# Down stage of a transformer block: loads ordered by hand on one queue, operands two products ahead, and a warmed start

## Chip, cores, metric

One core of a Trainium2 chip. The metric is the device time of one launch in microseconds (us). Profiles show the span from the first to the last instruction, which is about 1.8 us shorter than the time of the same execution.

## The reference

A block with linear attention and a gated feed-forward layer, batch 1, 2048 tokens, width 1024, hidden width 3584, all in bf16:

```python
h  = x + linear_attention(layernorm(x), wqkv) @ wo      # 32 heads of 32
g  = layernorm(h)
gate, up = g @ W_gate, g @ W_up
h2 = h + (gate * (gate > 0) * up) @ W_down              # the "down stage" is this product
```

## The kernel before

All large products use Strassen's scheme, seven products for eight. The down stage does it on two levels. Outside there are seven products of halves. Two of them are "plain" (112 matmuls of 512 columns, 24.2 us); five are "inner", that is again seven groups of 28 matmuls of 256 columns (3.06 us a group, 21.4 us in all). VectorE makes the operand sums of the next inner product (`t1` to `t4` from weights, `s1` to `s4` from hidden activations) between its other work: a *snapshot* adds a base to the running accumulator, a *sink* adds a finished accumulator to a snapshot, adds h and sends it out.

```python
OUTER = (1, 2, 6, 5, 7, 3, 4)
INNER = (2, 6, 5, 3, 4)          # 1 and 7 are plain
...
    def acc(tag):                # PSUM: A twice, X and Y once, two banks each
        return accs.tile([P, 2 * NW], FP32, tag=tag, bufs=2 if tag == "A" else 1, name="acc" + tag)
...
            cur["m1"]()
            ...
            cur["s1"]()          # snapshot of group 1
            cur["m2"]()
            if prv: prv["m4"]()  # groups of the product before, left over
            late_x()
            cur["00"]()          # sink of group 2
            pop()                # one operand sum of the next product
            ...
            late_w()
            pop()
            cur["m6"]()
            if prv: prv["01"]()
            pop()
            cur["m5"]()
            cur["s2"]()          # snapshot of group 6: frees the accumulator for group 7
            pop(2)
            cur["m7"]()
            pop(2)
            if tail:             # the last product
                cur["snap"]("u3", 1, 1)
                cur["snap"]("u3f", 1, 0)
                cur["m4f"]()
                cur["11"]()
                cur["m3"]()
                cur["10f"]()
                cur["01a"]()
                cur["01b"]()
```

Loads, h loads too, are issued from SyncE's queue when the scheduler puts them there, one product ahead.

Of the kernel before, what the change touches and what calls it, by code (L numbers as in the profile page):

```python
# [31 lines left out]
def block_kernel(ctx: ExitStack, tc: tile.TileContext, x, wqkv, wo, wg, wu, wd, out, H: int):  # L32
    nc = tc.nc
    P = 128
# [44 lines left out]
    PE_T = 4  # L79
    XB, HB = 3, 2  # L80
# [129 lines left out]
    with ExitStack() as actx:  # L210
# [36 lines left out]
        def ln_T(t):  # L247
# [13 lines left out]
            xn = bwork.tile([P, D], BF16, tag="hn", bufs=HB, name="xn")  # L261
            nc.vector.scalar_tensor_tensor(out=nmr, in0=mv[:, 0:1], scalar=-1.0, in1=rstd, op0=ALU.mult, op1=ALU.mult)
            nc.scalar.activation(out=xn[:], in_=x_sb[:], func=ACT.Identity, bias=nmr, scale=rstd)
            if t not in atiles[:PE_T]:
                nc.sync.dma_start_transpose(out=xT[s][i][:, :, r:r + P], in_=xn[:])
                return
            for k in range(2):
                pt = pspool.tile([P, KH, P], BF16, tag="D", bufs=1, name="tp")
                for kc in range(KH):
                    nc.tensor.transpose(pt[:, kc, :], xn[:, (k * KH + kc) * P:(k * KH + kc + 1) * P], ident[:])  # L270
                (nc.scalar.copy if k else nc.vector.tensor_copy)(
                    out=xT[s][i][:, k * KH:(k + 1) * KH, r:r + P], in_=pt[:])
# [93 lines left out]
        ln_T(atiles[0])  # L366
# [42 lines left out]
    abpool = abctx.enter_context(tc.tile_pool(name="abpool", bufs=3, space=PSUM, side="right"))  # L409
# [21 lines left out]
    with tc.tile_pool(name="qwork0", bufs=2, side="right") as pool:  # L431
        qw.append(pool)
        for c in range(0, KH, 2):
            for _ in q_unit(0, c):
                pass
    xctx[0].close()
    q1ctx = ExitStack()
    qw.append(q1ctx.enter_context(tc.tile_pool(name="qwork1", bufs=2, side="right")))
# [7 lines left out]
    def new_hn(s):  # L446
        aops = mctx.enter_context(tc.tile_pool(name=f"aops{s}", bufs=1))
        hnT.append([aops.tile([P, KC, SW], BF16, name=f"hn{s}{i}") for i in range(2)])
        hns.append([aops.tile([P, KH, SW], FP16, name=f"hs{s}{k}") for k in range(3)])

    new_hn(0)
    wpool = mctx.enter_context(tc.tile_pool(name="wpool", bufs=2))
# [3 lines left out]
    def load_group(g):  # L456

        tiles, loads = [], []
        for nm, v in (("wg", wg_v), ("wu", wu_v)):
            w_sb = wpool.tile([P, KC, 2, GP * P], BF16, tag=nm, name=nm)  # L460
# [108 lines left out]
    tpool = mctx.enter_context(tc.tile_pool(name="tpool", bufs=2))  # L569
    mwork = mctx.enter_context(tc.tile_pool(name="mwork", bufs=2))  # L570
# [33 lines left out]
    def wd_sums(c):  # L604
# [4 lines left out]
        def load():  # L609
            st["raw"] = raw = spool[0].tile([P, 2, 2, D], BF16, tag="wraw", bufs=1, name="wraw")  # L610
            for k in range(2):
                nc.sync.dma_start(out=raw[:, k], in_=wd_k[:, k, 2 * c:2 * c + 2, :])
            st["b"] = [[raw[:, k, :, j * DW:(j + 1) * DW] for j in range(2)] for k in range(2)]

        def one():
            st["t"] = spool[0].tile([P, 4, 2, DW], FP16, tag="wt", bufs=1, name="wt")
# [14 lines left out]
        return [load, one, two, three, four]  # L631
# [21 lines left out]
    def early_sums(f):  # L653
# [10 lines left out]
        return [load, lambda: None, lambda: hh_sums_a(st[0], 0, f), lambda: hh_sums_b(st[0], 0, f)]  # L664
# [56 lines left out]
    prepool = ctx.enter_context(tc.tile_pool(name="prepool", side="right", **reuse))  # L721
# [61 lines left out]

    runs = [(early[f // GP], f, f % GP, [1]) for f in range(NE)]
    runs += [(g, g * GP + fi, fi, [0, 1]) for g in range(NE // GP, FH // GP) for fi in range(GP)]
    fill = [p for f in range(NE) for p in early_sums(f)] + [p for c in range(FH // 2) for p in wd_sums(c)]
# [23 lines left out]
    for r, (wt, f, fi, toks) in enumerate(runs):  # L810
        w = [ops() for _, ops in now]
        later = []
        for n, s in enumerate(toks):
# [8 lines left out]
            if r >= NE:  # L822
                want = len(fill) // (nwin - k) if nwin - k > 1 else len(fill)
                want = min(len(fill), max(want, 0))
# [41 lines left out]
            if k == nwin - 1:  # L866
                b11 = [prepool.tile([P, FQ, DW], BF16, tag="b11", name="b11")]
                nc.sync.dma_start(out=b11[0][:], in_=wd_v[:, 0:FQ, 0:DW])
    assert not fill

    HW = DW // 2
    raws = {1: (0, 0), 2: (1, 0), 3: (1, 1)}
    sums_of = {4: 3, 5: 0, 6: 1, 7: 2}
    xslot = {2: H12, 3: S4, 4: H22, 5: S1, 6: S2, 7: S3}
    OUTER = (1, 2, 6, 5, 7, 3, 4)
    INNER = (2, 6, 5, 3, 4)
    outs = {2: (0, 0), 7: (1, 1), 3: (0, 1), 4: (1, 0)}
    full = slice(0, DW)
    ALL = slice(0, NT)

    def plain_mm(ps, x, w, p, kh):
        s, t0 = divmod(2 * p, NT)
        for t in range(2):
            for f in range(FQ):
                nc.tensor.matmul(ps[:, t * NW:(t + 1) * NW], lhsT=x[s][kh][:, f, (t0 + t) * P:(t0 + t + 1) * P],  # L885
                                 rhs=w[kh][:, f, :], start=(kh == 0 and f == 0),
                                 stop=(kh == 1 and f == FQ - 1), skip_group_check=True)

    first_ps = [acc("A")]
    wfirst = [b11[0][:], None]  # L890
    xfirst = [[t[:] for t in row] for row in x1]
    plain_mm(first_ps[0], xfirst, wfirst, 0, 0)
# [11 lines left out]
    dpool = ctx.enter_context(tc.tile_pool(name="dpool", **reuse))  # L904

    def load_half(op, x):

        k = op["k"]
        w = dpool.tile([P, FQ, DW], BF16, tag="w", bufs=4, name="w")
        if k in raws:  # L910
            i, j = raws[k]
            nc.sync.dma_start(out=w[:], in_=wd_v[:, i * FH + x * FQ:i * FH + (x + 1) * FQ, j * DW:(j + 1) * DW])
        else:
            nc.sync.dma_start(out=w[:].bitcast(FP16), in_=t_dram[sums_of[k]][:, x * FQ:(x + 1) * FQ, :])
        op["wt"][x] = w
        op["w"][x] = w[:] if k in raws else w[:].bitcast(FP16)

    def load_x(op, s, kh):

        k = op["k"]  # L920
        t = (x1pool if op["n"] % 2 == 0 else dpool).tile([P, FQ, SW], BF16, tag="x", bufs=4, name="x")
        nc.sync.dma_start(out=t[:], in_=x_dram[s][kh][:, xslot[k], :, :])
        op["xt"][s][kh] = t
        op["x"][s][kh] = t[:].bitcast(FP16) if k in (3, 5, 6, 7) else t[:]

    def new_op(n):
        return {"n": n, "k": OUTER[n], "wt": [None] * 2, "w": [None] * 2,
                "xt": [[None] * 2 for _ in range(2)], "x": [[None] * 2 for _ in range(2)], "s": {}, "t": {}}

    queue = []  # L930
# [10 lines left out]
    def queue_sums(op):  # L941
# [4 lines left out]
        def a(i, j):  # L946
            return op["x"][i][j]

        def b(i, j):
            return op["w"][i][:, :, j * HW:(j + 1) * HW]  # L950

        def new_s(nm):
            S[nm] = dpool.tile([P, FQ, SW], FP16, tag="xs", bufs=4, name="xs")[:]
# [11 lines left out]
        def t3():  # L965
            T["t3"] = op["wt"][0][:].bitcast(FP16)[:, :, HW:DW]
# [11 lines left out]
        def s3():  # L978
            S["s3"] = op["xt"][1][0][:].bitcast(FP16)
# [5 lines left out]
        queue.extend((op, f.__name__, f) for f in (t1, s1, s2, t2, s3, t3, t4, s4))  # L985
# [8 lines left out]
    def load_h(k, s):  # L994

        if k in outs:
            i, j = outs[k]
            v = dpool.tile([P, NT, DW], BF16, tag="h", bufs=3, name="h")
            nc.sync.dma_start(out=v[:], in_=h_dram[i][s][:, :, j * DW:(j + 1) * DW])
            hres[k, s] = v  # L1000

    def put(k, s, ts, cs, ps, m):

        i, j = outs[k]
        o = dpool.tile([P, NT * HW], BF16, tag="o", bufs=3, name="o")
        ov = o[:, 0:(ts.stop - ts.start) * (cs.stop - cs.start)].rearrange("p (t d) -> p t d", t=ts.stop - ts.start)
        add(out=ov, in0=ps, in1=m, op=ALU.add)  # L1007
        add(out=ov, in0=ov, in1=hres[k, s][:, ts, cs], op=ALU.add)
# [9 lines left out]
    def inner(op):  # L1018
# [4 lines left out]
        def left(m):  # L1023
            return {1: op["x"][0][0], 2: op["x"][0][1], 3: op["s"].get("s4"), 4: op["x"][1][1],
                    5: op["s"].get("s1"), 6: op["s"].get("s2"), 7: op["s"].get("s3")}[m]

        def right(m):
            w = op["w"]
# [6 lines left out]
        def mm(m, nm, t=None):  # L1035
# [4 lines left out]
            for tt in range(NT):  # L1040
# [9 lines left out]
        def sink(s, j, nm, m, ts=ALL):  # L1050
# [3 lines left out]
            else:  # L1054
                put(k, s, ts, cols(j), view(nm)[:, ts], m)
# [8 lines left out]
            "01a": lambda: sink(0, 1, "E", "u2", slice(0, 2)), "01b": lambda: sink(0, 1, "E", "u2", slice(2, 4)),  # L1064
            "m7f": lambda: snap("u3f", 1, 0),
# [3 lines left out]
    op = ops[0]  # L1069
    op["w"][0], op["x"] = b11[0][:], xfirst  # L1070
    load_half(op, 1)
    for n in range(1, 2):
        load_half(ops[n], 0)
        load_half(ops[n], 1)
        for s, kh in ((1, 0), (1, 1), (0, 0), (0, 1)):
            load_x(ops[n], s, kh)
# [7 lines left out]
    for p in range(1, 4):  # L1084
        plain_mm(pss[p], op["x"], op["w"], p, 0)
    for p in range(4):
        plain_mm(pss[p], op["x"], op["w"], p, 1)
        sink1(p, pss[p])
        if p >= 1:
            pop(2)  # L1090
    load_h(OUTER[1], 0)
    load_h(OUTER[1], 1)
    pop(8)

    prv = None
    for n in range(1, len(OUTER)):
# [4 lines left out]
        def early_loads():  # L1101
            if nxt:
                load_half(nxt, 0)
                for s, kh in ((1, 0), (0, 0), (0, 1)):
                    load_x(nxt, s, kh)
                load_h(nxt["k"], 0)

        def late_x():
            if nxt:
                load_x(nxt, 1, 1)  # L1110

        def late_w():
            if nxt:
                load_half(nxt, 1)
                if nxt["k"] in INNER:
                    queue_sums(nxt)

        early_loads()
        if op["k"] in INNER:
# [21 lines left out]
            if nxt:  # L1141
                load_h(nxt["k"], 1)
            cur["m5"]()
            cur["s2"]()
            pop(2)
            cur["m7"]()
            pop(2)
            if tail:
                cur["snap"]("u3", 1, 1)
                cur["snap"]("u3f", 1, 0)  # L1150
                cur["m4f"]()
                cur["11"]()
                cur["m3"]()
                cur["10f"]()
                cur["01a"]()
                cur["01b"]()
# [3 lines left out]
        else:  # L1160
            pss = []
            for p in range(4):
                ps = acc(("A", "A", "XY"[n % 2], "XY"[(n + 1) % 2])[p])
                plain_mm(ps, op["x"], op["w"], p, 0)
                plain_mm(ps, op["x"], op["w"], p, 1)
                if p == 0 and prv:
# [6 lines left out]
                    prv["01"]()  # L1173
                s, t0 = divmod(2 * p, NT)
# [5 lines left out]
            if nxt:  # L1180
                load_h(nxt["k"], 1)
# [47 lines left out]
```

## Time and profile before

| | before |
|---|---|
| time, median of 3 | 763.67 us (763.53 to 764.01) |
| profiled execution | 762.83 us, span 761.0 us, mean clock 0.996 |
| TensorE busy | 721.2 us, 95% |
| first matmul of the down stage | 583.74 us |
| last matmul ends, last addition of VectorE ends | 755.6, 757.8 us |

The prediction shows the lines that bear on the start and the down stage. Two more rows of TensorE's timeline are needed later, from the stretch where attention hands over to gate and up (start, length, engine, line, output and inputs, shape, count, and in brackets the wait before it with what ended it; a row without brackets followed its predecessor without a wait):

```profile
272.38 1.02 PE L673 MATMUL Aq<-hs,tu 128*128 128x512 f16 x4 [1.65 <-ACT m L152]
...
297.12 1.03 PE L753 MATMUL accA<-hn,wg 128*128 128x512 bf16 x4
```

The second is the first matmul of the main gate and up stage. From there to 583 us TensorE never waits as long as 0.4 us, so a lead or a lag at 297 us is carried to the down stage unchanged.

### The profile page before, as it was taken

The numbers are of one execution on the slowest core, as the hardware profiler recorded it, in microseconds if no ns is written. First come the engines' busy times: TensorE is split into PE (matmuls) and PEld (weight loads), VectorE is DVE, ScalarE is ACT, GpSimd is POOL, SyncE is SP. The second block draws the span as 40 slices with busy tenths as digits, with TensorE's granted clock in tenths as the row PEclk, the third lists the DMA queues.
The fourth block names the chain that finished last, engine by engine and source line by source line (L and its number), as shares of the span: only waits on it lengthen the run. The fifth ranks groups of instructions, "written<-read, shape, count | busy, mean of one in ns | idle before, by whom it ended". The sixth has DMA issues, their size and how long they took to land.

```text
span 761.0 us, 10554 instructions
## 1 busy us (share of the span) xinstructions
PE 721.2 (95%) x3951; PEld 381.3 (50%) x4004; DVE 565.7 (74%) x1022; ACT 326.5 (43%) x597; POOL 6.1 (1%) x44
## 2 busy tenths in 40 slices
PE   5999999999889989999999999999999879999996
PEld 2443555444344434444444444444444358875685
DVE  5997654787896767687777877788776279947995
ACT  4876553878768554444444444444434010000000
POOL 0000000000000000000000000000000000000000
PEclk9999999999999999999999999999999999999999
DMA  9665002079767544166438356495543899967713
GB/s 318 153 138 152 1 1 107 5 165 224 193 160 183 121 118 145 42 180 185 147 105 246 102 157 221 165 279 178 177 172 122 292 405 333 362 236 255 266 29 97
DMA packets 146419, 132.03 MB, mean 173 GB/s; under 512 B 50880, under 2 KB 127936, under 8 KB 146368
## 3 DMA queue, kind: packets, MB, share of 16 engines
q1 hardware_dynamic: 138928, 127.16, 55.3%
q10 hardware_dynamic: 7440, 4.20, 1.9%
q8 instruction: 31, 0.51, 0.3%
q14 instruction: 20, 0.16, 0.1%
HBM read 79.95 MB, written 39.85 MB: 157 GB/s over the span
## 4 chain that ended last, share of the span: by engine, by line
PE 65%; DVE 16%; DMA 9%; ACT 5%; issue 2%; SPq 1%; POOL 0%; DVEq 0%; ACTq 0%
PE accA L753 22%; PE accX L753 8%; PE accY L753 8%; DMA x<-x_dram 5%; PE accA L1042 4%; PE attn L517 4%; PE Aq L285 3%; PE Aq L419 2%; PE Eq L285 2%; PE Aq L673 2%; PE accX L1042 2%; PE accY L1042 2%; DVE stats L254 2%; DVE o L1007 1%; DMA hn<-hn 1%
## 5 line engine op out<-in xcount | busy, mean ns | idle before, releaser
L763 ACT ACTIVATE gu<-gu 128x512 bf16<-128x512 bf16 x72 | 45.4, 631 | 122.3 <-DVE gu L762 122.3
L758 ACT COPY snap<-accA 128x1024 f32<-128x1024 f32 x72 | 72.7, 1010 | 44.9 <-PE accA L753 44.8
L517 PE MATMUL attn<-wo_mem,oT 128*128 128x512 bf16 x247 | 57.3, 379 | 4.1 <-DVE o_sb L497 3.4
L753 PEld LDWEIGHTS <-tg 128*128 128x128 f16 x384 | 37.6, 98 | 45.3
L753 PEld LDWEIGHTS <-tu 128*128 128x128 f16 x384 | 37.6, 98 | 45.3
L1042 PEld LDWEIGHTS <-x 128*128 128x128 f16 (+1 forms) x560 | 54.6, 98 | 9.9 <-DMA out_dram<-o 1.3
L152 ACT COPY u<-Aq 128x512 f32<-128x512 f32 x56 | 32.2, 581 | 44.9 <-PE Aq L285 21.3
L762 DVE TENSOR_TENSOR gu<-accY,snap 128x1024 bf16<-128x1024 f32 x36 | 43.9, 1220 | 10.2 <-ACT snap L758 10.2
L753 PE MATMUL accA<-hn,tg 128*128 128x512 f16 (+1 forms) x192 | 49.3, 379 | 0.0
L753 PE MATMUL accA<-hn,tu 128*128 128x512 f16 (+1 forms) x192 | 49.3, 379 | 0.0
L762 DVE TENSOR_TENSOR gu<-accX,snap 128x1024 bf16<-128x1024 f32 x36 | 43.9, 1220 | 7.0 <-ACT snap L758 3.9
L1042 PEld LDWEIGHTS <-xs 128*128 128x128 f16 x420 | 41.7, 99 | 11.1 <-issue 5.7
L753 PEld LDWEIGHTS <-wg 128*128 128x128 bf16 x288 | 28.2, 98 | 34.0
L753 PEld LDWEIGHTS <-wu 128*128 128x128 bf16 x288 | 28.2, 98 | 34.0
L517 PEld LDWEIGHTS <-oT 128*128 128x128 bf16 x256 | 24.9, 97 | 34.9 <-issue 6.7
L885 PEld LDWEIGHTS <-x 128*128 128x128 bf16 (+1 forms) x224 | 21.9, 98 | 29.2 <-issue 3.3
L1042 PE MATMUL accA<-w,x 128*128 128x256 f16 (+1 forms) x280 | 31.7, 273 | 1.0 <-DVE snap L1048 0.7
L766 DVE TENSOR_TENSOR hq<-gu 128x512 bf16<-128x512 bf16 x48 | 20.3, 423 | 14.9 <-ACT gu L763 14.9
L285 PEld LDWEIGHTS <-xT 128*128 128x128 bf16 (+1 forms) x192 | 18.6, 98 | 24.9 <-issue 3.4
L497 DVE TENSOR_TENSOR o_sb<-nd,rd 128x384 bf16<-128x384 f32 (+1 forms) x48 | 22.8, 507 | 8.6 <-ACT rd L496 8.3
L1048 DVE TENSOR_TENSOR snap<-accA,u 128x1024 f32<-128x1024 f32 x16 | 19.4, 1219 | 11.5 <-PE accA L1042 11.5
L519 DVE SCALAR_TENSOR_TENSOR x_res<-attn,x_res 128x512 bf16<-128x512 f32 x32 | 22.0, 688 | 6.3 <-PE attn L517 6.2
(199 smaller groups left out, 1368.4 us busy)
## 6 DMA issues: line engine op xcount, KB each, us to landing
x<-x_dram SPq DMA_DIRECT2D x24, 896.0 KB, 7.2
x_dram<-hq SPq DMA_DIRECT2D x28, 512.0 KB, 3.1
wg<-in_B_W_gate_dram SPq DMA_DIRECT2D x14, 512.0 KB, 5.0
wu<-in_B_W_up_dram SPq DMA_DIRECT2D x14, 512.0 KB, 7.2
wraw<-in_B_W_down_dram SPq DMA_DIRECT2D x14, 512.0 KB, 4.9
x_dram<-hq SPq DMA_DIRECT2D x28, 256.0 KB, 3.0
t_dram<-wt SPq DMA_DIRECT2D x28, 256.0 KB, 2.2
w<-t_dram SPq DMA_DIRECT2D x8, 896.0 KB, 8.4
```

The costliest lines, as they stand in the source:

```text
L152: nc.scalar.copy(out=snaps[nm, v], in_=A[v][:])
L285: nc.tensor.matmul(ps[:], lhsT=left[m - 1][:, kc, r + v * P:r + (v + 1) * P], rhs=right[m - 1][:, kc, :], start=(start and kc == 0), stop= ...
L497: nc.vector.tensor_tensor(out=ov[:, c0:c0 + n], in0=ndv[:, :, 0:P].rearrange("p k (h e) -> p k h e", h=HPC), in1=rd[:, 0:n, :].unsqueeze(3 ...
L517: nc.tensor.matmul(ps[:], lhsT=st["oT"][:, c, :], rhs=wo_sb[:, c, j * NW:(j + 1) * NW], start=(c == 0), stop=(c == KC - 1))
L519: nc.vector.scalar_tensor_tensor(out=h_sb[:, j * NW:(j + 1) * NW], in0=ps[:], scalar=1.0, in1=h_sb[:, j * NW:(j + 1) * NW], op0=ALU.mult, ...
L753: nc.tensor.matmul(ps[:, v, :], lhsT=w[v][n - 1][:, kc, :], rhs=left[n - 1][:, kc, :], start=(t is not None and kc == 0), stop=(kc == KH - ...
L758: nc.scalar.copy(out=st[nm][:], in_=halves(st["A"]))
L762: add(out=g[:], in0=halves(st[nm]), in1=st[base][:], op=ALU.add)
L763: nc.scalar.activation(out=g[:, 0, :], in_=g[:, 0, :], func=ACT.Relu)
L766: add(out=out[q], in0=st[q][:, 0, :], in1=st[q][:, 1, :], op=ALU.mult)
L885: nc.tensor.matmul(ps[:, t * NW:(t + 1) * NW], lhsT=x[s][kh][:, f, (t0 + t) * P:(t0 + t + 1) * P], rhs=w[kh][:, f, :], start=(kh == 0 and ...
L1042: nc.tensor.matmul(pv[:, tt, :], lhsT=left(m)[:, f, tt * P:(tt + 1) * P], rhs=right(m)[:, f, :], start=(t is not None and f == 0 and tt % ...
```

## The change

The intent: no load on the path of the down stage. Its parts, cut to the core:

```diff
 # start
+        with tc.high_priority():
+            zero = asmall.tile([P, NW], BF16, tag="zero", bufs=1, name="zero")
+            nc.vector.memset(zero[:], 0.0)
+            spin = pspool.tile([P, NW], FP32, tag="E", bufs=2, name="spin")
+            for n in range(16):
+                nc.tensor.matmul(spin[:], lhsT=zero[:, 0:P], rhs=zero[:], start=True, stop=True)
+            ln_T(atiles[0])        # first tile: normalised on VectorE in two halves
 # pools of the middle: waits tile by tile; staging of the weight sums in two buffers
-    mwork = mctx.enter_context(tc.tile_pool(name="mwork", bufs=2))
+    mwork = mctx.enter_context(tc.tile_pool(name="mwork", reuse_waits="tile", bufs=2))
-            st["raw"] = raw = spool[0].tile([P, 2, 2, D], BF16, tag="wraw", bufs=1, name="wraw")
+            raw = fpool.tile([P, 4 * D], BF16, tag="wraw", bufs=2, name="wraw")[:].rearrange(...)
 # down stage
-    OUTER = (1, 2, 6, 5, 7, 3, 4)
+    OUTER = (1, 2, 6, 5, 3, 7, 4)
+    ctx.enter_context(tc.manual_schedule(engines={ET.SP}))      # loads in the order written
-        queue.extend(... (t1, s1, s2, t2, s3, t3, t4, s4))
+        queue.extend(... (t1, s1, s2, t2, s4, s3, t3, t4))
-            nc.sync.dma_start(out=v[:], in_=h_dram[i][s][...])
+            nc.scalar.dma_start(out=v[:], in_=h_dram[i][s][...])
+        def ahead():                                            # x of the product after next
+            if n + 2 < len(OUTER):
+                need(op, "s4"); load_x(n + 2, 0, 0); load_x(n + 2, 0, 1)
 # last product: the last group in two halves, h added to its snapshot ahead
-                cur["m3"]()
-                cur["10f"]()
-                cur["01a"]()
-                cur["01b"]()
+                cur["m3a"]()
+                cur["10f"]()
+                cur["01a"]()
+                cur["m3b"]()
+                cur["01b"]()
```

Both halves of the first plain product's weights are also loaded some two windows of gate and up earlier, in place of one half shortly before.

## The prediction

> **What bounds the kernel now.** I read the page's busy shares first, then busy time by stretch, then TensorE's waits, then TensorE's timeline in the last quarter, then the queue's timeline there.
>
> ```profile
> PE 721.2 (95%) x3951; PEld 381.3 (50%) x4004; DVE 565.7 (74%) x1022; ACT 326.5 (43%) x597; POOL 6.1 (1%) x44
> ```
>
> TensorE is idle for 761.0 - 721.2 = 39.8 us, so nothing that only removes waits can win more than about 5%. The stretches say where those 40 us lie (columns: stretch, its length, then busy us and count of TensorE, weight loads, VectorE, ScalarE, GpSimd, then clock, DMA share, GB/s):
>
> ```profile
> 0.00:20.00 20.00, 11.12 (x57) 5.44 (x59) 12.25 (x27) 9.84 (x18) 1.84 (x23) 1.00 0.97 322
> 20.00:40.00 20.00, 19.89 (x98) 9.25 (x99) 19.90 (x50) 16.09 (x34) 0.00 (x0) 1.00 0.70 147
> ...
> 400.00:500.00 100.00, 99.53 (x457) 45.30 (x463) 77.33 (x143) 42.81 (x58) 0.00 (x0) 1.00 0.59 180
> ...
> 600.00:625.00 25.00, 18.48 (x111) 10.87 (x112) 13.09 (x9) 4.05 (x4) 0.00 (x0) 0.99 1.05 395
> 625.00:650.00 25.00, 24.88 (x216) 21.72 (x216) 23.84 (x21) 0.00 (x0) 0.00 (x0) 0.94 0.94 340
> ```
>
> Gate and up (300 to 583 us) are full and cannot gain. The start loses 8.9 us; the stretches between 40 and 300 lose some 14, and its waits are for VectorE and ScalarE results in program order. The down stage, from 583.7, is where the diff works. TensorE's timeline (start, length, line, count, in brackets the wait before):
>
> ```profile
> 602.48 6.20 PE L885 MATMUL accA<-w,x 128*128 128x512 bf16 x28 [3.03 <-DMA w<-in_B_W_down_dram]
> ...
> 618.07 3.22 PE L1042 MATMUL accY<-w,x 128*128 128x256 bf16 x28
> 625.12 4.56 PE L1042 MATMUL accA<-ws,xs 128*128 128x256 f16 x28 [3.83 <-DVE snap L1048]
> 629.52 3.22 PE L1042 MATMUL accY<-ws,xs 128*128 128x256 f16 x28
> ...
> 713.38 3.22 PE L1042 MATMUL accY<-w,x 128*128 128x256 bf16 x28 [1.09 <-DMA out_dram<-o]
> ...
> 752.37 3.22 PE L1042 MATMUL accX<-w,xs 128*128 128x256 f16 x28 [0.52 <-DVE o L1007]
> ```
>
> 28 matmuls of 256 columns follow one another at 3.06 us (736.40, 739.46, 742.51 in the same view), 28 of 512 columns at 6.05. The stage is 16 leftover matmuls of gate/up (3.46 us), two plain products of 4 x 6.05 = 24.2, five inner products of 7 x 3.06 = 21.4: 158.9 us, so without waits its last matmul would end at 583.74 + 158.9 = 742.6. It ends at 755.6. The 13.0 us between are eight waits (3.03, 0.27, 3.83, 0.20, 1.09, 0.80, 0.51, 0.52, together 10.25), 4.56 - 3.22 = 1.34 us of slow clock, and about 0.17 us of drain at each wait. The wait of 3.83 is put down to a snapshot, but VectorE did that late because it had itself stood behind loads:
>
> ```profile
> 615.03 2.03 DVE L976 TENSOR_TENSOR xs<-xs,x 128x3584 f16<-128x3584 f16 x1 [0.86 <-DMA x<-x_dram]
> 594.48 4.20 SPq L912 DMA_DIRECT2D w<-in_B_W_down_dram  x3
> 598.72 4.52 SPq L922 DMA_DIRECT2D x<-x_dram  x4
> 607.73 7.61 SPq L922 DMA_DIRECT2D x<-x_dram  x3
> ```
>
> Seven transfers of 896 KB, 6.3 MB, are issued only from 594.5 on and need about 16 us at 395 GB/s. The end of the chain is VectorE's (757.8) plus 3.2 us for the last store.
>
> **What the Trainium skill says.** (1) "TensorE: Matmul & The Clock Gate", Part 1: an idle window of about 3.4 us halves the clock, and about 3.4 us of work restores it. The trace agrees: 3.83 us idle is followed by the 4.56 us row, 3.03 us is not. (2) "DMA: Bandwidth & Descriptors", Issuing engines are not separate DMA queues: a second issuing engine gives no bandwidth, only issue time. So moving the h loads to ScalarE's queue must not be counted as faster transfers. (3) The same page, Anatomy of one DMA: a semaphore wait is done by the issuing sequencer before dispatch. So a load whose buffer is not free holds everything behind it; the 7.61 us row for three issues agrees. (4) "VectorE: DVE Perf Modes", the perf-mode tier table: a two-tensor operation runs at 2x on 16-bit SBUF data, at 1x on fp32 or PSUM. The trace agrees (2.02 us for 3584 16-bit elements, 1.22 for 1024 fp32), and it makes VectorE the next bound.
>
> **The change, part by part.** The instruction orders differ on TensorE only in the 16 zero matmuls at the start, in the first tiles' order, and in the down stage; the middle of VectorE and ScalarE has the same order.
>
> *Start.* 16 zero matmuls warm the clock and the first tile is normalised on VectorE. The three first projection matmuls took 1.48 us (0.43 apart), later ones 0.216, so some 9 slow ones cost about 1.9 us. But the copy of the first transposed tile still stands behind the second tile's statistics, whose input lands at 7.3 us, and VectorE is 99.5% busy from 20 to 40. What I can follow through VectorE is its idle 0.77 us at 14.5. I take **-0.8 us**.
>
> *Per-tile pool waits, staging doubled.* No wait in the list is a pool boundary, and gate/up has 1 us idle in all: **0**.
>
> *First plain product.* Both halves of its weights are loaded some two windows earlier, the wait of 3.03 goes. It then runs 583.74 + 3.46 + 24.2 = 611.4, unbroken.
>
> *First inner product's operands.* Two of four x tiles are loaded before the stage. The rest still stands in the queue behind the store of the last hidden tile (594.07), but it is 3.6 MB, not 6.3, and ends near 605 instead of 615. VectorE's eight sums (4 x 1.94 + 4 x 1.0 = 11.8) end near 612.5, and the second sums are needed at 617.5. The waits 0.27 and 3.83, and the slow clock, go.
>
> *New wait 1.* VectorE's new order puts, after the first sink (617.7 to 619.6), t1, s1 and s2 of the next product (1.0 + 1.94 + 1.94) and the 1.15 us snapshot: 625.6. The fifth group of matmuls cannot overwrite the accumulator before; it could have begun at 611.4 + 12.2 = 623.6. **+2.05**. Then 628.7 is the next start, and three products follow at 21.4: the walk down VectorE's order finds each snapshot 0.5 to 1 us ahead of need. The plain product now stands sixth and starts at T0 = 692.9.
>
> *New wait 2.* During it VectorE does the sinks of the product before (two of them and their h sums, to T0 + 14.2), four times put, h and add (1.25 + 0.61 + 1.13 = 3.0) and six of eight sums, to T0 + 35.9. The last product's second group needs the accumulator freed then, and could have come at T0 + 33.35: **+2.65**.
>
> *Tail.* Groups follow at 3.06 with the last split in two; h is added to the snapshot ahead, so one half-size add (0.69) remains. VectorE's list ends at T0 + 55.9, last matmul at T0 + 54.45. End of the span: 692.9 + 55.9 + 3.2 = 752.0. That is 9.0 below 761.0: 8.3 of it in matmuls, 0.7 in the tail.
>
> Sum: -9.0 - 0.8 = -9.8 on 763.67, about **753.8 us** (1.3%).
>
> **Rivals.** *A: VectorE takes the place of the loads, more than I count.* For: an inner product that writes output costs it 11.8 + 3 x 1.15 + 4 x 1.86 = 22.7 us against TensorE's 21.4, and 23.84 of 25 us were busy in 625 to 650. Against: two products write no output, and the reordering puts a product without following sums before the plain one. If snapshots come 0.5 to 1 us late in each product: 757. *B: my two new waits don't come*, because the sums of each product finish earlier than I walk them, and the start keeps all its 1.9 us: 763.67 - 9.0 - 4.7 - 1.9 = 748. Against: both waits follow from a fixed order and measured lengths. *C: the loads are late all the same.* An inner product's operands are 6 x 0.9 = 5.4 MB in 21.4 us, 251 GB/s, where 395 was reached; for it speaks that each load waits in order for a buffer, so one late release holds the rest. A hole of over 3.4 us with its slow clock would give 4 to 5 us back: 758.
>
> **Range and chances.** A and C end at 757 to 758, B at 748; a central 753.8 with 750 to 758 should hold it. Over 2% needs 748.4 or less, which only B in full reaches: 0.09. Slower by 2% would need a hang-like new wait of 25 us: 0.01.
>
> **What will show it.** Right: no TensorE wait for a load after 583; first inner product starting at 611 to 612 with the clock at 1.00 in 600 to 650; a wait of about 2 us before the fifth group of the first inner product and of 2 to 3 us before the second group of the last, both released by VectorE; 4 to 5 us from the last matmul to the end. Wrong: a wait over 3 us for x or w; a start that moves the middle of the kernel by over 2 us either way; or VectorE waits in every product.

## The result, and the profile after

| | before | after |
|---|---|---|
| time, median (executions) | 763.6 us (4) | **758.53 us** (4: 756.10, 758.53, 758.98, 758.54) |
| mean granted clock of these | – | 0.998, 0.995, 0.992, 0.995 |
| profiled execution | 762.83 us, span 761.0 | 756.10 us, span 754.3 |
| first matmul of the down stage | 583.74 | 583.71 |
| last addition of VectorE ends | 757.8 | 751.1 |

The ratio is 0.9932 with a 95% interval of 0.9905 to 0.9959. The change is 0.7% faster, not the 1.3% predicted, and 758.53 lies 0.5 us outside the range. The execution that was profiled is the fastest of the four.

Stretches of the changed kernel (length, then busy us and count of TensorE, weight loads, VectorE, ScalarE, GpSimd, then clock, DMA share, GB/s), to be held against those in the prediction:

```profile
0.00:20.00 20.00, 17.38 (x82) 7.68 (x84) 14.10 (x32) 9.98 (x19) 1.85 (x23) 1.00 0.97 324
600.00:625.00 25.00, 23.68 (x165) 16.05 (x164) 20.28 (x15) 4.05 (x4) 0.00 (x0) 1.00 0.97 366
625.00:650.00 25.00, 24.16 (x222) 21.64 (x222) 24.56 (x21) 0.00 (x0) 0.00 (x0) 1.00 0.85 311
```

The down stage is as intended: 600 to 625 us went from 18.48 to 23.68 us of busy TensorE, and no wait for a load is left after 583 us. What waits TensorE still has there, and two rows of the middle, from its timeline:

```profile
270.06 1.86 PE L693 MATMUL Aq<-hs,tu 128*128 128x512 f16 x4 [2.22 <-ACT m L153]
...
297.09 1.02 PE L773 MATMUL accA<-hn,wg 128*128 128x512 bf16 x4 [0.78 <-DVE gu L702]
...
625.84 3.22 PE L1105 MATMUL accA<-w,xd 128*128 128x256 f16 x28 [2.11 <-DVE snap L1111]
729.20 3.22 PE L1105 MATMUL accX<-wd,x 128*128 128x256 f16 x28 [2.61 <-issue]
748.70 1.69 PE L1105 MATMUL accX<-wd,xd 128*128 128x256 f16 x14 [2.49 <-DVE o L1069]
```

The reader sees the two new waits of the prediction (2.11 us at 625.84, 2.61 us at 729.20), and three things that it did not have. The row at 270.06 takes 1.86 us where the same four matmuls took 1.02: half clock, that is, the record of the granted clock reads 0.50 there, for 3.41 us. The row at 297.09 waits where before it did not. And the last 14 matmuls wait 2.49 us. Those are the second half of the last group; VectorE's last rows show what they wait for:

```profile
747.35 0.69 DVE L1071 TENSOR_TENSOR o<-o,h 128x1024 bf16<-128x1024 bf16 x1
747.96 0.68 DVE L1069 TENSOR_TENSOR o<-accX,snap 128x512 bf16<-128x512 f32 x1
750.42 0.69 DVE L1069 TENSOR_TENSOR o<-accX,snap 128x512 bf16<-128x512 f32 x1 [1.78 <-PE accX L1105]
```

The addition from 747.96 to 748.64 reads the *first* half of the accumulator; the matmuls of the second half begin 0.06 us later, though they write the other half.

### The profile page after: what moved, and what is told of

Its sections match the earlier page's. It is cut to its first block, busy times and chain, and to the rows that moved or that the text cites. A ratio compares the mean times of both kernels' runs of the same rounds, so it can differ in the third digit from the quotient of the medians.

```text
span 754.3 us, 10598 instructions
## 1 busy us (share of the span) xinstructions
PE 726.0 (96%) x3967; PEld 382.8 (51%) x4020; DVE 567.4 (75%) x1023; ACT 324.5 (43%) x596; POOL 5.8 (1%) x44
## 5 line engine op out<-in xcount | busy, mean ns | idle before, releaser
L1105 PEld LDWEIGHTS <-x 128*128 128x128 f16 (+1 forms) x448 | 43.8, 98 | 8.3 <-issue 2.9
L1105 PEld LDWEIGHTS <-xs 128*128 128x128 f16 x308 | 30.1, 98 | 3.5
L934 PEld LDWEIGHTS <-x 128*128 128x128 bf16 (+1 forms) x168 | 16.5, 98 | 19.8
L1105 PEld LDWEIGHTS <-xd 128*128 128x128 f16 (+1 forms) x224 | 21.9, 98 | 7.7 <-issue 5.0
```

The source lines that it names most:

```text
L1105: nc.tensor.matmul(pv[:, tt, :], lhsT=left(m)[:, f, tt * P:(tt + 1) * P], rhs=right(m)[:, f, :], start=(t is not None and f == 0 and tt % ...
```

## The experiments

Twelve kernels, each timed in five rounds against the kernel before on the same chip, four to a chip (after_again, start_only, no_start and spin_d on one; tail_order, wait1, wait2 and all4 on a second; the rest on a third). "After" below is the changed kernel. Medians, with the ratio to the kernel before (762.89 us on the first chip, 763.12 on each of the other two). A difference between medians of two chips is only as good as these ratios:

| kernel | edit to | median us | lowest to highest | mean clocks | ratio, 95% |
|---|---|---|---|---|---|
| after_again | none | 758.46 | 756.82 to 760.77 | 0.989 to 0.998 | 0.9942 [0.9926, 0.9958] |
| filled | after | 756.52 | 755.67 to 757.61 | 0.995 to 0.998 | 0.9917 [0.9893, 0.9942] |
| start_only | before | 762.92 | 761.13 to 766.22 | 0.989 to 0.997 | 1.0008 [0.9986, 1.0029] |
| no_start | after | 758.95 | 755.57 to 763.15 | 0.987 to 1.000 | 0.9944 [0.9919, 0.9970] |
| spin_d | after | 759.10 | 755.27 to 761.87 | 0.987 to 0.998 | 0.9943 [0.9920, 0.9967] |
| tail_order | after | 757.18 | 754.77 to 759.21 | 0.993 to 0.997 | 0.9921 [0.9898, 0.9944] |
| wait1 | after | 759.24 | 756.51 to 760.25 | 0.991 to 0.995 | 0.9942 [0.9922, 0.9962] |
| wait2 | after | 756.30 | 754.53 to 757.61 | 0.992 to 0.997 | 0.9908 [0.9890, 0.9927] |
| old_order | after | 761.67 | 760.47 to 763.69 | 0.992 to 0.995 | 0.9985 [0.9961, 1.0009] |
| h_sync | after | 760.25 | 757.59 to 763.27 | 0.989 to 0.995 | 0.9968 [0.9940, 0.9995] |
| all4 | after | 751.11 | 749.63 to 752.86 | 0.995 to 0.998 | 0.9847 [0.9826, 0.9868] |
| five | after | **749.15** | 748.72 to 749.99 | 0.996 to 0.999 | 0.9821 [0.9797, 0.9844] |

### The clock: after_again and filled

`after_again` is the changed kernel without an edit.

> The changed kernel unaltered, to see its spread. Its profiled execution took 756.1 us with a mean granted clock of 0.998, its three timed ones 758.5 to 759.0 us with 0.992 to 0.995. My theory: the 2.4 us between them are further windows of half clock (each 3.41 us long, so 1.7 us lost, 0.002 of the mean clock), which come or not with their phase against the waits of 2.1 to 2.6 us. Then time and mean clock go together: executions near 0.998 take 756 us, near 0.995 758 to 758.5, near 0.992 759 to 760. Rival: the difference is something else (loads landing at another time), and executions of the same mean clock differ by 2 us or more.

Its ten executions, those of the first result included, in order of mean clock: 0.998: 756.10, 756.82, 757.09. 0.995: 758.35, 758.53, 758.54, 758.57. 0.992: 758.98. 0.991: 759.49. 0.989: 760.77. Time and mean clock fall in one order, and executions of one clock lie within 1.0 us. So most of this spread is half clock, and the profiled execution was fast because it had little of it. Mean clock does not settle everything: filled has 755.67 and 757.56 us at 0.997, all4 749.63 and 751.11 us at 0.998, and the kernel before 761.33 and 763.12 us at 0.996 on one chip.

The profile of this run was taken of a slower execution (759.49 us) and shows what the fast one lacks. First the stretches around the wait of 2.6 us in the execution of 756.10 us, cut at the limits of the clock's records, then the same in this one (the clock is the third number from the end):

```profile
727.43:730.84 3.41, 1.64 (x16) 1.50 (x16) 3.41 (x4) 0.00 (x0) 0.00 (x0) 1.00 0.48 154
730.84:734.26 3.42, 3.42 (x34) 3.04 (x32) 3.16 (x4) 0.00 (x0) 0.00 (x0) 1.00 0.67 230
```

```profile
727.38:730.80 3.42, 0.97 (x9) 0.91 (x10) 3.39 (x5) 0.00 (x0) 0.00 (x0) 1.00 0.32 92
730.80:734.21 3.41, 3.41 (x18) 2.43 (x16) 2.06 (x2) 0.00 (x0) 0.00 (x0) 0.50 0.92 289
```

The wait is as long in both, 2.61 and 2.62 us. In the first it is split by the limit of two stretches, 1.77 us of idle in one of them (3.41 - 1.64), and nothing follows. In the second 2.44 us fall in one stretch, and the next one runs at half clock. Its matmuls, from its timeline:

```profile
729.83 4.88 PE L1105 MATMUL accX<-wd,x 128*128 128x256 f16 x28 [2.62 <-issue]
...
750.95 2.86 PE L1105 MATMUL accX<-wd,xd 128*128 128x256 f16 x14 [2.49 <-DVE o L1069]
```

4.88 us in place of 3.22: such a window costs 1.66 us, and the last 14 matmuls pay for one as well (2.86 in place of 1.69).

I cut all fourteen profiles (the two first ones and the twelve runs) into stretches of 3.413 us, on the grid that each profile's own clock records give, from 30 us to the last matmul. Windows of one profile lie whole multiples apart (in that of after, 270.05 and 754.74 us are 142.0 apart), so the grid runs free of the kernel. There are 24 stretches with 1.96 us or more of idle TensorE: all 24 are followed by half clock. Of some 2,900 with 1.95 us or less, only one at full clock is (it has 1.949 us); one more was at half clock already (start_only, 602.09). The idle time of a stretch can come from several waits: two of 1.79 and 0.90 us near 202 us share a stretch, in whole or in part, in the seven of the fourteen profiles that go to half clock there. This is a count over traces and not an experiment on the mechanism; the experiment is `filled`. It gives TensorE something to do in the two waits of 2.1 and 2.6 us:

```diff
-            for tt in ts:
+            for tt in ([0, 1] if again else []) + list(ts):     # first half twice; it starts anew
...
-            "m1": lambda: mm(1, "A", "A"),
+            "m1": lambda: mm(1, "A", "A", again=(op["n"] == 6)),    # the last product
-            "m5": lambda: mm(5, "E", tag),
+            "m5": lambda: mm(5, "E", tag, again=(op["n"] == 1)),    # the first inner product
```

> The changed kernel with 14 matmuls done twice ahead of each of its two waits of the down stage (the first half of the fifth-last product's group before the 2.11 us wait, of the last product's first group before the 2.61 us wait; the repeat starts the accumulator anew, so the result stays). TensorE does 3.05 us more of work, but inside waits that VectorE ends. In the ten profiles so far each stretch of 3.41 us on a fixed grid with 1.96 us or more of idle TensorE was followed by half clock, and all but one of the stretches with 1.95 us or less were not. My theory: the waits shrink to about 0.6 and 1.1 us, the last product's second group starts at the same time as in the changed kernel, and no half clock window falls between 600 and 740 us in any execution. Of all executions so far some half had one there, so the median falls from 758.5 to about 757, with none below 755.5. Rival: half clock has nothing to do with these waits; then such windows stay in the profile, or the duplicates cost up to 3 us: 760 us or more.

("The fifth-last product" in that text means the first inner product.)

```profile
626.38 3.22 PE L1105 MATMUL accA<-w,xd 128*128 128x256 f16 x28 [0.59 <-DVE snap L1111]
...
729.75 3.22 PE L1105 MATMUL accX<-wd,x 128*128 128x256 f16 x28 [1.09 <-issue]
```

With 28 more matmuls the median *falls* by 1.9 us, to 756.52 (on another chip; the two ratios, 0.9942 and 0.9917, differ by as much, though their intervals overlap), and the waits are as expected, 0.59 and 1.09 us. In the profile no half clock lies between 209 and 754 us. No execution was below 755.5 (lowest 755.67). That no execution had such a window I cannot show, since only one has a trace; the lowest mean clock of six was 0.995 where that of after_again was 0.989.

### The start: start_only, no_start, spin_d

`start_only` puts the start of the change alone on the kernel before; `no_start` takes it alone out of the changed kernel. The instruction orders agree with before and after on every engine from 63 us on; up to there the start changes those of VectorE and ScalarE too.

> The kernel before with only the start of the change: 16 zero matmuls and the first tile normalised on VectorE. My theory: it wins about 3.4 us of TensorE's lead by 100 us, and by 297 us all of it is gone again (the waits for VectorE and ScalarE between 220 and 297 grow, and the first accumulator of gate and up waits for the tile E that the zero matmuls put first), so the down stage starts within 0.7 us of the kernel before's 583.7 and the time is 763 to 764 us like before. Rival: the lead reaches the end, and it was other parts of the change that cost it: then 760 us, and the down stage starts at about 580.5.

> The changed kernel without its start: no zero matmuls, first tile as in the kernel before, all else of the change kept. My theory: the start is worth nothing at 583 us, so the time is within 1 us of the changed kernel (756 to 759 us), there is no half-clock window near 270 us (before had none) and the wait ahead of the first accumulator of gate and up near 297 us is gone. Rival: the start is worth its 3.4 us, so 760 to 762 us.

`spin_d` is one word:

```diff
-            spin = pspool.tile([P, NW], FP32, tag="E", bufs=2, name="spin")
+            spin = pspool.tile([P, NW], FP32, tag="D", bufs=1, name="spin")
```

> The changed kernel with the zero matmuls writing a tile of tag D instead of E, the only edit; the orders of the engines stay, one wait on VectorE moves from the first to the third accumulator of gate and up. My theory: the tile E came first in its pool because of the zero matmuls, so the first accumulator lies where VectorE reads last. The wait of 0.78 us at 297.09 us goes, and the time falls by about 0.9 us against the changed kernel (755.2 us profiled, if the windows of half clock fall alike). Rival: the next accumulators wait instead, and nothing changes by more than 0.3 us.

The medians of start_only and of no_start equal those of before and after within 0.5 us: the start is worth nothing that can be timed. Where it goes, by the starts of the same four TensorE rows in each profile (all in us):

| kernel | start warmed | first nd that waits | Aq<-hs,tu | first accA of gate/up | down stage | half clock ahead of 297 us |
|---|---|---|---|---|---|---|
| before | no | 205.53 | 272.38 | 297.12 | 583.74 | none |
| no_start | no | 205.16 | 271.83 | 296.56 | 583.19 | none |
| start_only | yes | 202.97 | 270.69 | 297.74 | 584.36 | 271.00 |
| after | yes | 202.06 | 270.06 | 297.09 | 583.71 | 270.05 |
| wait1 | yes | 202.82 | 270.67 | 296.34 | 582.96 | none |
| spin_d | yes, tag D | 202.56 | 271.95 | 298.06 | 584.69 | 203.72, 271.99 |
| all4 | yes, tag D | 202.34 | 270.14 | 294.86 | 581.49 | none |

At 202 us the warmed kernels lead by 2.6 to 3.5 us. (In a profile not listed, wait2's, it is only 0.9.) By 272 us 1.0 to 1.2 us of it is gone where no half clock came in between (wait1, all4, and after up to its window): the rows in between wait longer for VectorE and ScalarE. The wait before Aq<-hs,tu is one of them, 1.33 us in no_start and 1.65 in before, but 1.8 to 2.2 us with the start, which from 1.96 us in one stretch on is enough for a half clock window:

```profile
271.83 1.02 PE L687 MATMUL Aq<-hs,tu 128*128 128x512 f16 x4 [1.33 <-ACT m L153]
...
296.56 1.03 PE L767 MATMUL accA<-hn,wg 128*128 128x512 bf16 x4
```

```profile
271.95 1.87 PE L693 MATMUL Aq<-hs,tu 128*128 128x512 f16 x4 [1.98 <-ACT m L153]
...
298.06 1.03 PE L773 MATMUL accA<-hn,wg 128*128 128x512 bf16 x4
```

The first fence is no_start, the second spin_d. In spin_d, which has the warmed start, the wait of 0.78 us at accA is gone, as in no_start and all4; it stands in start_only, after_again, tail_order, wait1, wait2 and all others with tag E. So that wait is the zero matmuls' doing. How is read from the program and not from a trace: their tile comes first in its pool and takes tag E to the front of PSUM, where the first accumulator of gate and up is put afterwards and has to wait for VectorE's last read of it. In time spin_d shows nothing (median 759.10 us). In its profiled execution (761.56 us) two half clock windows ahead of 297 us, 3.3 us, hide a gain of 0.9; for the others there is no trace. Comparing profiles without such windows: the start is worth 296.56 - 296.34 = 0.2 us with tag E (no_start, wait1) and 296.56 - 294.86 = 1.7 us with tag D (no_start, all4; 0.5 us of it is a lead that all4 has over wait1 at 202 us already).

### The tail: tail_order

```diff
                 cur["m3a"]()
+                cur["m3b"]()
                 cur["10f"]()
                 cur["01a"]()
-                cur["m3b"]()
                 cur["01b"]()
```

> The changed kernel with the second half of the last group of matmuls issued in program order before the two stores of the tail instead of between them; the order on each engine stays, TensorE loses one wait on VectorE. My theory: the 2.49 us wait ahead of the last 14 matmuls is a wait for a read of the other half of the same accumulator tile. It goes, VectorE's last two half-size additions follow its others at once (from 748.0 us in the profile of the changed kernel, 0.69 us each) and the end comes 1.8 us earlier at full clock, a little more on average because a half clock window after this wait goes too: about 756.5 us. Rival: VectorE alone sets the end there, and the gain is below 0.7 us.

The orders of the engines stay the same; in the compiled program TensorE loses one wait on VectorE, and VectorE's last addition one on TensorE.

```profile
749.36 0.69 DVE L1071 TENSOR_TENSOR o<-o,h 128x1024 bf16<-128x1024 bf16 x1
749.97 1.28 DVE L1069 TENSOR_TENSOR o<-accX,snap 128x512 bf16<-128x512 f32 x2
```

Then the last group of TensorE:

```profile
746.52 3.22 PE L1105 MATMUL accX<-wd,xd 128*128 128x256 f16 x28
```

In tail_order the two half-size additions follow the rest at once, and all 28 matmuls of the last group follow their predecessors. The wait is gone. From the start of the last product's second group (731.21 in tail_order, 729.20 in after) to the last addition's end it is 20.04 us, where after has 21.91: 1.9 us won, 1.8 expected. The rival, below 0.7 us, falls. The median, 757.18 us, is 1.3 us below after_again's, measured in another set of rounds; half clock windows of the middle, two of them in this profile, spread the executions over 4.4 us.

### The two waits: wait1 and wait2

`wait1` moves two operand sums behind the snapshot in the first inner product:

```diff
-            pop()                       # after late_w, and again after 01
+            if n > 1:
+                pop()
             ...
             cur["s2"]()
-            pop(2)
+            pop(2 if n > 1 else 4)
```

> The changed kernel with one reordering on VectorE: in the first inner product the second snapshot comes ahead of two of the next product's operand sums (s1, s2) instead of behind them. My theory: the 2.11 us wait at 625.8 us goes (below 0.3 us), no other wait of over 0.5 us takes its place, and the last product starts 2.0 us earlier; with the half clock windows that follow this wait in some executions, about 756 us. Rival: VectorE was 23.84 of 25 us busy here in the kernel before, so the sums now come late instead: the wait moves to the next product and under 0.7 us is won.

```profile
645.47 3.22 PE L1105 MATMUL accA<-wd,x 128*128 128x256 f16 x28 [0.85 <-DVE snap L1111]
```

The wait of 2.11 us is gone, and one of 0.85 us stands in the next product at the same snapshot: 1.26 us net, between my theory and the rival. VectorE is nearly full here (24.56 of 25 us from 625 us on in after), so a sum moved away from one snapshot falls on the next. The median (759.24 us) doesn't show the gain; the wait of 2.62 us and the tail's each had its half clock window in the profile, and mean clocks were 0.991 to 0.995.

`wait2` swaps two accumulators of the plain product and leaves two sums for later:

```diff
-                ps = acc(("A", "A", "XY"[n % 2], "XY"[(n + 1) % 2])[p])
+                ps = acc(("A", "A", "XY"[(n + 1) % 2], "XY"[n % 2])[p])
...
-                pop(2)
+                if p < 3:
+                    pop(2)
```

> The changed kernel with the last two accumulators of the plain product swapped and two sums moved from behind its last quarter into the last product. My theory: the 2.61 us wait ahead of the last product's second group is for the accumulator that the last quarter's addition on VectorE frees; with the third quarter's instead it goes (below 0.3 us), and the last matmul comes 2.4 us earlier; about 755.7 us with the half clock windows that go with it. The tail wait of 2.49 us stays. Rival: the tail's additions on VectorE are what ends the kernel, and the two sums moved there take the gain back: under 1 us.

```profile
728.85 3.22 PE L1105 MATMUL accX<-wd,x 128*128 128x256 f16 x28
732.72 3.22 PE L1105 MATMUL accA<-ws,xs 128*128 128x256 f16 x28 [0.65 <-DVE snap L1111]
```

The wait of 2.61 us is gone; a wait of 0.65 us for a snapshot came one group later, which I had not expected. Against after_again the median fell by 2.2 us, to 756.30 us (expected 755.7). The tail's wait stayed at 2.49 us.

### Parts undone: old_order and h_sync

`old_order` sets `OUTER = (1, 2, 6, 5, 7, 3, 4)` again in the changed kernel (with one h load moved so that it is there).

> The changed kernel with the outer products in the order of the kernel before (1, 2, 6, 5, 7, 3, 4), and one h load moved where it is needed for it. My theory: VectorE then has two products with outputs after one another at the end, 22.7 us of work each against 21.4 on TensorE, and the waits that the kernel before has there (1.09, 0.80, 0.51 us) come back beside the one of 2.6 us, which moves to the product after the plain one: 2 us slower than the changed kernel, about 760.5. Rival: the order is worth nothing, because the waits of before came from late stores and loads: within 0.7 us of the changed kernel.

```profile
707.77 3.22 PE L1105 MATMUL accY<-w,x 128*128 128x256 bf16 x28 [2.02 <-issue]
...
719.87 4.88 PE L1105 MATMUL accA<-w,xd 128*128 128x256 f16 x28 [2.73 <-DVE snap L1111]
```

761.67 us, 3.2 us slower than after_again. The size of the waits is as expected, 2.02 + 2.73 in place of 2.61, 2.1 us more, but not their places: not the three small waits of before, but one large one at a snapshot, with its half clock window (4.88 us). So undoing the order alone gives back 3.2 us of the 4.4 us that after_again has over before (two chips). More than that: in old_order TensorE has no wait for a load after 583 us, and still the kernel cannot be told from the kernel before (0.9985, 0.9961 to 1.0009). With the old order, taking the loads off the path bought nothing measurable: waits that VectorE ends took their place.

`h_sync` issues the h loads from SyncE's queue again:

```diff
-            nc.scalar.dma_start(out=v[:], in_=h_dram[i][s][:, :, j * DW:(j + 1) * DW])
+            nc.sync.dma_start(out=v[:], in_=h_dram[i][s][:, :, j * DW:(j + 1) * DW])
```

> The changed kernel with the h loads issued from the queue of the operand loads again. My theory: operands are loaded two products ahead, so a load held behind an h load that waits for its buffer has time to spare: no new TensorE wait over 0.3 us, time within 0.7 us of the changed kernel at equal clock (756 to 759). Rival: the separate queue is what keeps the operand loads on time; then a wait for x or w of 1 us or more shows after 640 us, and 760 us or more.

A row of VectorE's timeline, then one of TensorE's:

```profile
621.62 2.03 DVE L1035 TENSOR_TENSOR xs<-x 128x3584 f16<-128x3584 f16 x1 [0.66 <-DMA x<-x_dram]
```

```profile
626.95 3.22 PE L1105 MATMUL accA<-w,xd 128*128 128x256 f16 x28 [2.86 <-DVE snap L1111]
```

Neither expectation holds in full: the median, 760.25 us, is what the rival said, but its wait after 640 us did not come. An operand sum waits 0.66 us for its x, and TensorE's first wait grows from 2.11 to 2.86 us: 0.75 us, more than my 0.3 and less than the rival's 1.0. The x that this sum needs is issued at the same place in both kernels (611.53 us in after, 611.89 in h_sync, whose stage lies 0.36 us later) but lands at 619.02 and at 621.53 us. In h_sync the second h load lands ahead of it (619.34), in after behind it (626.07), while some 400 GB/s are moved in both. So what the second queue seems to have changed is which bytes came first, not how many. The median is 1.8 us above after_again's; at equal mean clock four of six executions lie within 0.8 us of after_again's, so part of it is half clock coming more often (mean clocks 0.989 to 0.995). How large a part is not settled.

### Together: all4 and five

`all4` is spin_d, tail_order, wait1 and wait2 together.

> The changed kernel with four edits together: zero matmuls on tag D, the tail's order, and the two above. My theory: the parts add up, 0.9 + 1.8 + 2.0 + 2.4 = 7.1 us at equal clock, and since no wait of over 1 us is left after 300 us, no half clock window falls there except at the very end; windows near 203 and 271 us stay possible. Median about 749.8 us, all executions within 748 and 752.5. Rival: half clock windows come whatever the waits, and the median is 751.5 or more with windows after 600 us.

751.11 us, 1.5% faster than before. Executions lie between 749.63 and 752.86 us, one of five above the 752.5 expected; my 749.8 was low by 1.3 us. Waits of 1.15 us (at 644.30) and 0.65 us (at 727.35) were left, which I had not counted; but the profiled execution, which has them, took 749.63 us, so they don't explain why the median is higher. `five` takes the first of them away, in the second inner product as wait1 did in the first:

```diff
-            if n > 1:
+            if n > 2:
                 pop()                            # the one after 01
...
-            pop(2 if n > 1 else 4)
+            pop({1: 4, 2: 3}.get(n, 2))
```

> The kernel with four edits together (751.1 us) and a fifth: in the second inner product, too, the second snapshot comes ahead of an operand sum. My theory: the wait of 1.15 us at 644.3 us goes, VectorE catches up in the product without output that follows, and the time falls by 0.8 to 1.1 us, to about 750.1. Rival: VectorE has no slack left, and the wait comes back in the next product: 751 us.

```profile
727.53 3.22 PE L1105 MATMUL accA<-ws,xs 128*128 128x256 f16 x28 [0.64 <-DVE snap L1111]
```

This is the only wait of over 0.4 us that TensorE has left after 297 us. The median is 749.15 us, 2.0 us below all4 (on another chip), and all five executions lie within 1.3 us. From the first matmul of the down stage to VectorE's last addition the profiles show 161.9 us against all4's 162.9: the 1.0 us expected. The other 1.0 us is not explained. It beats before (ratio 0.9821, 14 us) and after (by 9.3 us between medians).

## Why the prediction was wrong, point by point

**The plain product, the loads, new waits 1 and 2, the order: right.** First inner product at 611.34 (said 611.4), first wait 2.11 us (2.05), second 2.61 us (2.65), the plain product at 693.09 (692.9, or 692.1 with the start's 0.8), no wait for a load. The operands were later than said (last x at 608.5 us for "near 605", VectorE's sums done at 615.4 for "near 612.5") and still 2 us ahead of need. Four of the five signs named as right came (the fifth, 4 to 5 us from the last matmul to the end, was 3.9); wait1 and wait2 removed the two waits by what the prediction gave as their causes. Rival C did not come, and B was wrong on both counts. Rival A is true in kind, though not in "each product": wait1 and old_order show VectorE as what takes the place of the loads in this stage.

**The tail: the step that failed most in the profile.** "Groups follow at 3.06 with the last split in two" and "VectorE's list ends at T0 + 55.9" left out that the second half, as the program is ordered, has to wait for the read of the first half, 2.49 us. VectorE ended at 693.09 + 58.0. tail_order shows it: 1.9 us.

**The start: -0.8 us was 0.** It was too small at 100 us (3.5 us) and too large at the end. The warmed start leads by 3.5 us at 202 us in the profiled execution, and none of it is left at 297 us: 1.1 us went in longer waits to 272 us, 1.7 us in a half clock window that one of them set off, 0.3 us came back near 283 us, and 0.9 us went in the wait of the first accumulator. start_only and no_start show the zero, spin_d and all4 the accumulator. "A start that moves the middle of the kernel by over 2 us" stood among the signs of a wrong prediction.

**Half clock: the rule was wrong.** "3.83 us idle is followed by the 4.56 us row, 3.03 us is not" was read as a threshold near 3.4 us of wait. In these traces what counts is the idle part of a stretch on a fixed grid, and 1.96 us is enough. It sorts these two rows as well: the wait of 3.83 us puts 3.20 us of idle into one stretch, the wait of 3.03 us is split and puts at most 1.88 us into one. Waits of 2.0 to 2.6 us therefore cost up to 1.66 us more in a part of the executions. The prediction counted its two new waits at their bare length and the clock at 1.00.

The sum: in the profiled execution the span should have been 752.0 - 0.8 = 751.2 us and was 754.3. Of the 3.1 us, 1.0 is the later plain product (0.8 start, 0.2 the walk) and 2.1 the tail. The medians are 4.7 us apart (758.5 against 753.8); the remaining 1.6 us is that the changed kernel's typical execution is 2.4 us slower than its profiled one, at 0.995 against 0.998 of the clock, while for the kernel before that difference is 0.8 us (763.67 against 762.83). The mechanism of the gain was right; the misses are two terms that were wrong and one that was left out.

**Not settled.** The loads ordered by hand and issued two products ahead, the core of the change, were not undone by themselves; that they took the load waits away is read from the traces (TensorE has no wait for a load after 583 us in after or in any kernel made from it). Why the row at 270 us waits up to 0.6 us longer when TensorE comes early is only read from the trace. The per-tile pool waits were not run alone; in no_start, which has them and no warmed start, the lead over before stays between 0.2 and 0.6 us from 205 us to 583 us, so with all else that differs ahead of the down stage they are worth no more than that.

## What to carry to other kernels

On this kernel a wait of TensorE of 2 us or more cost its length and, in a part of the executions, up to 1.7 us more. Keeping the idle time of every stretch of 3.41 us below 1.9 us, if need be with useless matmuls, took the second part away; two short waits close together count as one. A new tile at the head of a pool can move every tile behind it; look at the waits of the stage that later takes over the memory. Before taking one engine's waits away, add up the next engine's work in the same stage: here VectorE stood behind the loads. When several small edits each drown in the spread, compare the profiles wait by wait, and time them together.

## What the Trainium skill lacked or had wrong

- "TensorE: Matmul & The Clock Gate", Part 1, gives the idle state as coming "after ≥1 idle window (~3.4µs)". Here a grid stretch of 3.41 us was followed by half clock whenever 1.96 us of it was idle (24 of 24 in fourteen profiles); the 2.22 us wait at 270.06 was enough. That the window runs free and lasts 3.41 us agrees with the traces (two windows 142.0 lengths apart). No page that I read gives the idle share that is enough. A window cost 1.66 us (4.88 against 3.22 us for 28 matmuls), in a part of the executions only; executions of after_again spread over 4 us (756.8 to 760.8).
- No page that I read has the remedy: with 28 needless matmuls inside two waits the median was 1.9 us lower (filled, 756.52 against 758.46 us).
- "DMA: Bandwidth & Descriptors", Issuing engines are not separate DMA queues, agrees with the traces as to bandwidth (some 400 GB/s with one queue and with two, h_sync and after). It does not say that the second queue can change what lands first: the x load landed at 621.5 us behind the h load with one queue and at 619.0 ahead of it with two, and TensorE's wait in the first inner product was 2.86 against 2.11 us.
- No page that I read says that a wait can be kept for a whole accumulator of two banks when the two accesses touch different halves: 2.49 us in the tail (tail_order removes it by program order alone).
